# One core, attention and a gated feed-forward layer: the last batch's keys and queries turned over by DMA, four forms of products told apart by the planner, the fourth batch's scores in steps of four banks

## The chip, the core and the metric

The kernel runs on one core of one Trainium2 chip. A core has five engines that run their own streams of instructions and wait for each other by semaphores: TensorE (PE: matmuls, with PEld for the loading of its weights), VectorE (DVE), ScalarE (ACT), GpSimd (POOL) and SyncE (SP, which here only issues DMAs). The metric is the device time of one launch in microseconds. The kernel before took 404.94 us (median of 3 runs, 404.52 to 405.55).

## What is computed

Attention for 8 batches of 8 heads, 576 tokens of 64 features, with 16 "beacon" keys and values in front that every token sees; then a feed-forward layer with a gate on all 4608 tokens of 512 features.

```python
k_all = np.concatenate([beacon_k, k], axis=2)          # q, k, v: 8 x 8 x 576 x 64; beacons: 16 rows
scores = scale * np.matmul(q, k_all.transpose(0, 1, 3, 2))
scores = np.where(causal, -1000000000.0, scores)       # beacons are seen by all
a = softmax(scores)
x = np.matmul(a, v_all)                                # then heads side by side: 4608 x 512
gate = np.maximum(x @ w_gate, 0.0)                     # 512 x 1536
val = x @ w_val
out = gate * val @ w_out                               # 1536 x 512
```

All inputs and the output are float32 in the chip's main memory (HBM); products are made in bf16.

## The kernel before

**The order is worked out by a planner.** The kernel's Python text first describes its work as a list of tasks (`add`, L178), each with the engines that may run it, a cost in us, the tasks that it needs, the buffers that it holds and a priority. `Plan.order` (L186) then plays them against those costs and writes the instructions out in the order that comes of it; so each engine's stream is fixed, and on the chip the engines only wait for what they need. For each task the planner knows the earliest time `at` at which it could run. It takes the smallest `at`; among equals a mark called `late`, and then the priority. For TensorE `late` (L232) depends on the task's form, `part`: a task of the same form as the one before goes first (-1), and one that changes the form waits behind others (1) until it has been ready for `lazy` us. A change of form costs `SWITCH` in the plan.

**Forms.** TensorE's array is used whole (128*128) for the feed-forward products, for turnings (transposes as matmuls with an identity) and for fillers; in quarters (64*64) for scores; in halves (128*64) for values; and 128*32 for the scores of the last rows. The tasks carry `part=2` for scores (L751), `part=1` for values (L868) and for the last rows' scores (L796), and 0 for the rest. The values of the last rows (L862, "F") are whole-array products but carry 1 too. Values have `lazy=20` from the third batch on.

**Attention, batch by batch** (`new_batch` L493, `quad` L763, `last` L784). The 8 heads are 4 pairs; a quad is 2 pairs, so a batch has quads 0 and 1. Keys and queries of a pair come by one DMA on SP's queue in runs of 1 KB (four rows of 64 floats; L554), are rounded to bf16 on POOL (L514), turned over by four 128-column matmuls (L525) into a PSUM bank, and copied by ACT or DVE into the tiles `kT` or `qT` (L463, L465). The first 16 rows and the rows left over come by loads of their own (L607), values by rows in 256-byte runs (L644). Scores (L743) are made in steps that hold PSUM banks: `STEPS` has six small steps to a quad, `STEPS2` three large ones of four banks (two for each of two heads); `BIGSTEP` (L34) says from which batch on `STEPS2` is used: before, from batch 4, the fifth. Then the softmax: masks and minima on DVE (L691), exponentials on ACT (L698), reciprocals on DVE (L704), scaling on POOL (L709). The weights are turned over by a DMA transpose on SP's queue (L829), for the first batch by matmuls (L819); then come the values (L839, L862) and copies into `xT`, from which the feed-forward part reads.

**Feed-forward** (`ffn` L892). Tokens are taken in ten spans (240, 336, seven of 512, 448). For each, 12 times: gate (L900) and value (L905), four matmuls each; ACT takes the relu (L911), DVE the product (L916); then 12 matmuls for each 128 tokens give the output (L931), which is copied to one of three `osb` tiles and stored by SP (L945). A span begins when the attention of all its tokens is in `xT`.

**What sets the order at the start.** POOL issues nine weight DMAs (`weight` L475; 512 KB each in bf16 at the destination, 1 MB of float32 read), not before `W0` + `W_STEP` times their number in plan time (L479). `HELD` (L38) keeps a load of the second batch, and those after it, behind the issue of a weight: the entry `(1, 3): ('v', 0, 0)` holds load 3 of batch 1 until the first w_val piece has been issued, through a one-element memset on POOL (L535). The loads' order in a batch is "KQ0011v2233vvvv" (L651): 0 and 1 are rests, 2 and 3 pair 0, 4 and 5 pair 1. `BEHIND` (L39) holds a load behind the scaling of a quad. `AFTER` and `PACE` (L61, L62) set the plan time from which a quad's scores may run: with 39, quad g of batch b from 39 * (b + g/2) on. Where the plan leaves TensorE idle before 160 us, fillers (L990), products that nobody reads, are put in.

Of the kernel before, what the change touches and what calls it, by code (L numbers as in the profile page):

```python
# [17 lines left out]


BACKLOG = 4.0  # L20
RANK1 = -10.0
AHEAD = 2.0
WWORK = -15.0
FILLED = 160.0
# [5 lines left out]
LAGS = {"PE": 0.22, "ACT": 0.16, "DVE": 0.14, "POOL": 0.1, "DMA": 0.1}  # L30
LAZY = 20.0
LAZY1 = 0.0
ON_PE = 2
BIGSTEP = 3  # L34
PEQ = lambda b, g: b < 1
ENG = [("POOL", "DVE"), ("POOL",), ("POOL",)]
F_MOST = 3
HELD = {(1, 3): ('v', 0, 0), (1, 5): ('g', 0, 512), (1, 11): ('o', 0, 0)}  # L38
BEHIND = {(2, 7): (1, 1)}  # L39
MARK = 0.08  # L40
AB_FIRST = 0
W_FIRST = 0
# [4 lines left out]
ORDER0 = ("k00", "q00", "K", "Q", "k10", "q10", "v", "v", "k01", "q01", "k11", "q11", "v", "v", "v")  # L47
W_COLS = [(0, 512), (512, 512), (1024, 512)]
W_ROWS = 4
W0 = 16.5  # L50
W_STEP = 3.4
W_ISSUE = 0.85
W_MOVE = 0.72
V_MOVE = 1.25
LAND = 1.8
N_ST = 8
N_OSB = 3
FIRST_SPANS = [240, 336]
LAST_SPAN = 448
FIRST_MOST = 3  # L60
AFTER = [[0.0, 8.0]]  # L61
PACE = 39.0  # L62


class Slots:
# [104 lines left out]
class Plan:  # L170
# [7 lines left out]
    def add(self, engines, cost, run, deps=(), holds=(), prio=0.0, lag=None, part=0, lazy=0.0, after=0.0, move=0.0):  # L178
        t = Task(engines if isinstance(engines, tuple) else (engines,), cost, run, deps, holds, prio, lag, part, lazy, move)
        t.ready = after  # L180
        for d in t.deps:
            d.users.append(t)
        self.tasks.append(t)
        return t

    def order(self):  # L186
# [11 lines left out]
        part = 0  # L198
# [23 lines left out]
        while True:  # L222
            best = None
            for e in queue:
                for t in queue[e]:
                    times = begin(t, e)
                    if times is None:
                        continue
                    at, could = times
                    late = 0  # L230
                    if e == "PE":
                        late = -1 if part and t.part == part else 1 if part != t.part and at < t.ready + t.lazy else 0  # L232
                    key = (at, late, t.prio)
                    if best is None or key < best[0]:
                        best = (key, t, e)
            if best is None:
                break
            (at, _, _), t, e = best
            for x in t.engines:
                queue[x].remove(t)  # L240
            for h in t.holds:
                if h.tile is None:
                    if h.next is not None:
                        h.tile, h.next.tile = h.slots.take_pair()
                    else:
                        h.tile = h.slots.take()
            if e == "PE" and FILL_FROM < at < self.filled:
                since, tile = max(free[e], FILL_FROM), self.filler
                if at >= FILL_BANK:
                    first = min(self.banks.free, key=lambda f: f[:2], default=(at, 0, None))  # L250
                    since, tile = max(since, first[0]), first[2]
                n = int((at - since) * FILL / (0.11 if at > FILL_COLD else 0.22))
                if n > 0 and tile is not None:
                    done.append(Filler(n, tile, self.fill))
            t.start, t.engine = at, e
            cost = t.cost
            if e == "DMA":
                issue, move = cost
                if issue > 1.2:
                    wire = max(wire, at + 0.3) + move  # L260
                    free[e] = max(at + issue, wire - 0.2)
                else:
                    free[e] = at + issue
                    wire = max(wire, at + issue) + move
                end = max(wire, free[e]) + LAND
            else:
                if isinstance(cost, dict):
                    cost = cost[e]
                if e == "PE":
                    cost += SWITCH * (t.part != part)  # L270
                    part = t.part
                free[e] = end = at + cost
                if t.move:
                    wire = max(wire, end) + t.move
                    end = wire + LAND
            for h in t.holds:
                h.users -= 1
                if h.users == 0:
                    h.slots.give(end + (0.1 if e == "DMA" else LAGS[e] if t.lag is None else t.lag), h.tile)
            done.append(t)  # L280
            for u, then in [(u, end) for u in t.users] + [(u, free[e]) for u in t.soon]:
# [11 lines left out]
def kernel(  # L293
# [12 lines left out]
    nc = tc.nc  # L306
    B, H, S, D = q.shape
    Nb = beacon_k.shape[2]
    DM = H * D
    NT = B * S  # L310
# [182 lines left out]
    def new_batch(b, prio, work):  # L493
# [24 lines left out]
        def turned(h16, rows, ca, prio):  # L518
            ps = Hold(first_ps if b == 0 else v_ps, 2)

            def turn(_):
                for a in range(4):

                    to = ps.tile[:, a * P:a * P + rows]
                    nc.tensor.matmul(to, h16.tile[:rows, a * P:(a + 1) * P], ident[:rows, :rows], start=True, stop=True)  # L525

            return ps, add("PE", c_pe(4 * rows), turn, (ca, on_ident), (h16, ps), prio[1])
# [20 lines left out]
        def load_pair(kind, p, prio):  # L548

            src, s0 = {"k": (k, 0), "q": (q, 64 - Nb)}[kind]  # L550
            st = staged()

            def fetch(_):
                nc.sync.dma_start(st.tile.rearrange("p (h e) -> p h e", h=2),  # L554
                                  src[b, bass.ds(4 * (p // 2) + p % 2, 2, step=2), s0:s0 + MAIN, :].rearrange("h (p j) d -> p h (j d)", j=4))

            ld = add("DMA", (0.5, 0.87), fetch, (held,), (st,), prio[0])
            dst = t.kT if kind == "k" else t.q
            h16, ca = rounded(dst, st, P, neg_scale if kind == "q" else 1.0, prio, ld,
                              lambda to, src: [(  # L560
                to.rearrange("p (j h d) -> p h j d", h=2, j=4), src.rearrange("p (h j d) -> p h j d", h=2, j=4))])
            zeros = on_zeros.get(b) if kind == "q" else None
            ps, tu = turned(h16, P, ca, prio)
            c0 = Nb if kind == "k" else 64
# [149 lines left out]
    def quad_scores(t, g, step, phs, vals, prio, after):  # L714
# [34 lines left out]
        for x in banks[0] + banks[1]:  # L749
            x.users += 1  # L750
        s = add("PE", sum(x[2] for x in cols) / 2400.0 + 0.03, scores, deps, (*banks[0], *banks[1], *[phs[k] for k in ks], t.kT, t.q), prio, None,  # L751
                part=2, after=after)
        parts = [[], []]
        for k in ks:
            phs[k].users += 1
# [28 lines left out]
    def last(t, prio):  # L784

        ph = Hold(p_s[0], 1)
        sc = [Hold(first_sc if t.b == 0 else sc_s, 4) for _ in range(2)]
        sc[0].next, sc[1].prev = sc[1], sc[0]
        deps = [x for key, made in t.rows.items() if key[0] in "kq" for x in made]
        def scores(_):  # L790
            for bank, a, n in ((sc[0], 0, 512), (sc[1], 512, SK - 512)):
                for pp in range(NP):
                    nc.tensor.matmul(bank.tile[32 * pp:32 * pp + 32, :n], t.q.tile[:, pp, S + Nb - TAIL:],
                                     t.kT.tile[:, pp, a:a + n], start=True, stop=True)

        s = add("PE", SK / 2400.0 + 0.05, scores, deps, (*sc, ph, t.kT, t.q), prio, None, part=1)  # L796
        parts = [(SK, tuple(sc), 0, mask_f, SK - 512, on_mask_f, 0, s)]
        outs = softmax(t, parts, ph, prio, 0)
        ph.users += 1 + len(outs)
        finish(t, 0, ("F",), ph, pT_s[0], NC, [list(range(NC))] if t.b < ON_PE else [], outs, prio)  # L800

    def finish(t, p, vals, ph, pt_s, blocks, on_pe, outs, prio):
# [30 lines left out]
        def one(what):  # L833
# [8 lines left out]
            def values(_):  # L842
# [15 lines left out]
                else:  # L858
                    for pp in range(NP):
# [6 lines left out]
            nv = 2 if what == "AB" else NC  # L866
            pe = {"AB": 0.17, "CDE": 0.54, "F": 0.45}[what]
            va = add("PE", pe, values, tr + [t.rows["v", c] for c in range(nv)], (pt, ps, t.v), prio - 5, None,  # L868
                     part=1, lazy=LAZY if t.b > 1 else LAZY1 * t.b)

            def to_x(x):
                pv = ps.tile
# [99 lines left out]
    spans = []  # L972
    for w in FIRST_SPANS:
        spans.append((sum(spans[-1]) if spans else 0, w))
    end = NT - LAST_SPAN
    while sum(spans[-1]) < end:
        a = sum(spans[-1])
        spans.append((a, min(MT, end - a)))
    spans.append((end, NT - end))
    for i, (m0, mt) in enumerate(spans):  # L980
        deps = []
        for b in range(B):
# [41 lines left out]
```

## Time and profile before

| | us |
|---|---|
| median of 3 runs | 404.94 |
| lowest, highest | 404.52, 405.55 |
| the profiled execution | 405.02 |
| its span (first to last instruction) | 403.3 |
| PE busy | 388.6 |
| DVE, ACT, POOL busy | 294.8, 260.3, 233.9 |
| SP's DMA queue (q1): packet time as a share of 16 engines' span | 72.7% |

The profiled execution is 0.08 us above the median, and 1.7 us of it lie outside the span. Busy times are the union of an engine's instructions. Durations of matmuls overlap, since they are pipelined: what one costs is the distance from its start to the next one's.

### The profile page before, as it was taken

To read this page: it belongs to the slowest core of one execution; us is meant where nothing else is said; L and a number is where in the kernel's file an instruction comes from. 1 tells how busy PE (TensorE), PEld (TensorE's weight loads), DVE (VectorE), ACT (ScalarE), POOL (GpSimd) and SP (SyncE) were. 2 spreads that over 40 slices of the span, in tenths; PEclk is the share of its full clock that TensorE was granted. 3 is DMA by queue.
4 is the path that set the end of the run, shared out by engine and by line. 5 is a ranking of instruction groups with operands and counts; after the bars stand their busy time and mean duration, and the time that the engine had idled before them with its cause. 6 is when DMAs were issued, how large, how long until landed. Compare 5 with 4: busy or idle time off the path is not lost.

```text
span 403.3 us, 9980 instructions
## 1 busy us (share of the span) xinstructions
PE 388.6 (96%) x3276; PEld 205.8 (51%) x3316; DVE 294.8 (73%) x1046; ACT 260.3 (65%) x814; POOL 233.9 (58%) x453
## 2 busy tenths in 40 slices
PE   6999999999999999999999999999999999999994
PEld 4657855545444546455545444544454454444542
DVE  3899899896989897788797969797868633333331
ACT  2998798895877687769676878496848621320310
POOL 6899979796769469586758676676443320000000
PEclk9999999999999999999999999999999999999999
DMA  7999989999999999899999969792829074002002
GB/s 186 202 239 227 242 138 228 184 213 258 211 228 217 185 207 216 183 267 252 167 195 286 216 152 238 218 221 47 164 78 192 0 138 133 0 0 98 8 2 92
DMA packets 173476, 67.83 MB, mean 168 GB/s; under 512 B 145712, under 2 KB 168880, under 8 KB 173424
## 3 DMA queue, kind: packets, MB, share of 16 engines
q1 hardware_dynamic: 168592, 62.41, 72.7%
q0 software_dynamic: 4752, 4.72, 7.2%
q8 instruction: 26, 0.43, 0.4%
q14 instruction: 26, 0.21, 0.2%
q10 hardware_dynamic: 80, 0.07, 0.1%
HBM read 38.54 MB, written 9.44 MB: 119 GB/s over the span
## 4 chain that ended last, share of the span: by engine, by line
PE 85%; DMA 6%; POOL 3%; DVE 2%; ACT 1%; issue 1%; SPq 1%; DVEq 0%
PE f L931 23%; PE f L905 22%; PE f L900 21%; PE f L839 6%; PE f L743 6%; PE f L525 4%; DMA wv_r<-in_moe_w_val_dram 2%; DMA pTb<-pb 2%; POOL pb L709 1%; DMA st<-in_q_dram 1%; PE f L819 1%; ACT xT L698 1%; PE f L862 1%; PE f L990 1%; DVE f L691 1%
## 5 line engine op out<-in xcount | busy, mean ns | idle before, releaser
L709 POOL TENSOR_SCALAR pb<-pb,small 128x384 bf16<-128x384 bf16 (+8 forms) x272 | 141.5, 539 | 74.1 <-DVE small L704 73.4
L698 ACT ACTIVATE pb<-f,small 128x448 bf16<-128x448 f32 (+8 forms) x272 | 143.9, 554 | 27.4 <-DVE small L691 23.9
L691 DVE CUSTOM_DVE_ANT_0 f<-f,mask 128x576 f32<-128x576 f32 (+8 forms) x288 | 134.3, 513 | 13.6 <-PE f L743 9.6
L905 PE MATMUL f<-xT,wv_r 128*128 128x512 bf16 (+3 forms) x466 | 106.3, 358 | 2.3 <-DMA wv_r<-in_moe_w_val_dram 1.0
L900 PE MATMUL f<-xT,wg_r 128*128 128x512 bf16 (+3 forms) x471 | 105.2, 358 | 0.7 <-DMA wg_r<-in_moe_w_gate_dram 0.4
L916 DVE TENSOR_TENSOR hT<-g,f 128x512 bf16<-128x512 f32 (+3 forms) x120 | 75.1, 632 | 38.0 <-PE f L905 35.1
L911 ACT ACTIVATE g<-f 128x512 f32<-128x512 f32 (+3 forms) x120 | 67.0, 564 | 55.0 <-PE f L900 50.7
L931 PE MATMUL f<-wo_r,hT 128*128 128x512 bf16 (+3 forms) x439 | 98.8, 374 | 1.6 <-issue 1.1
L900 PEld LDWEIGHTS <-wg_r 128*128 128x128 bf16 x480 | 45.1, 98 | 44.3 <-issue 1.5
L905 PEld LDWEIGHTS <-wv_r 128*128 128x128 bf16 x480 | 43.8, 98 | 44.5 <-issue 5.1
L931 PEld LDWEIGHTS <-hT 128*128 128x128 bf16 (+2 forms) x456 | 41.9, 100 | 46.9 <-issue 2.9
L698 ACT ACTIVATION_READ_ACCUMULATOR pb<-f,small 128x1 f32 x272 | 60.8, 224 | 0.0
L514 POOL TENSOR_SCALAR h<-st 128x512 bf16<-128x512 f32 (+1 forms) x93 | 49.1, 542 | 12.1 <-DMA st<-in_k_dram 4.0
L691 DVE DVE_READ_ACCUMULATOR2_ANT small<- 128x1 f32 x296 | 41.9, 142 | 0.1
L465 DVE COPY osb<-f 128x512 f32<-128x512 f32 (+3 forms) x32 | 21.9, 683 | 26.1 <-PE f L931 25.9
L743 PE MATMUL f<-kT,qT 64*64 64x512 bf16 (+7 forms) x640 | 34.8, 295 | 0.1
L525 PE MATMUL f<-ident,h 128*128 128x128 bf16 (+1 forms) x320 | 28.1, 221 | 1.4 <-POOL h L514 1.2
L704 DVE RECIPROCAL small<-small 128x1 f32<-128x1 f32 (+3 forms) x144 | 22.0, 161 | 8.9 <-ACT pb L698 6.4
L525 PEld LDWEIGHTS <-h 128*128 128x128 bf16 (+1 forms) x320 | 21.3, 100 | 14.0 <-POOL h L514 3.2
L743 PEld LDWEIGHTS <-qT 64*64 64x64 bf16 x640 | 14.4, 106 | 23.1 <-issue 18.6
L839 PE MATMUL f<-pTb,v 128*64 128x320 bf16 (+3 forms) x488 | 25.7, 253 | 0.5 <-DMA pTb<-pb 0.5
L839 PEld LDWEIGHTS <-v 128*64 128x64 bf16 (+1 forms) x512 | 20.9, 109 | 8.9 <-issue 4.5
(61 smaller groups left out, 233.8 us busy)
## 6 DMA issues: line engine op xcount, KB each, us to landing
out_dram<-osb SPq DMA_DIRECT2D x34, 256.0 KB, 2.5
st<-in_k_dram SPq DMA_DIRECT2D x32, 256.0 KB, 4.1
st<-in_q_dram SPq DMA_DIRECT2D x32, 256.0 KB, 4.5
st<-in_v_dram SPq DMA_DIRECT2D x24, 256.0 KB, 5.8
st<-in_v_dram SPq DMA_DIRECT2D x8, 224.0 KB, 4.9
wg_r<-in_moe_w_gate_dram POOLq DMA_DIRECT2D x3, 512.0 KB, 7.4
wv_r<-in_moe_w_val_dram POOLq DMA_DIRECT2D x3, 512.0 KB, 7.6
wo_r<-in_moe_w_out_dram POOLq DMA_DIRECT2D x3, 512.0 KB, 7.6
```

Of the source, the lines that this page charges most:

```text
L514: (nc.gpsimd if x.engine == "POOL" else nc.vector).tensor_scalar(to, src, by, 1.0, ALU.mult, ALU.mult)
L525: nc.tensor.matmul(to, h16.tile[:rows, a * P:(a + 1) * P], ident[:rows, :rows], start=True, stop=True)
L691: nc.vector.tensor_tensor_reduce(out=view(i, n - m), in0=view(i, n - m), in1=msk, scale=1.0, scalar=at(7) if m < n else 3.0e38, op0=ALU.ad ...
L698: nc.scalar.activation(ph.tile.rearrange("p a n -> p (a n)")[:, a:a + n], view(i), AF.Exp, bias=at(i), scale=-1.0, accum_out=at(4 + i))
L709: nc.gpsimd.tensor_scalar(one, one, at(8 + i), 1.0, ALU.mult, ALU.mult)
L743: nc.tensor.matmul(banks[k][b_].tile[64 * i:64 * i + 64, off:off + n], t.q.tile[r, 2 * g + i, 64 * j:64 * j + 64], t.kT.tile[r, 2 * g + i, ...
L839: nc.tensor.matmul(ps.tile[64 * hh:64 * hh + 64, d0:d0 + w], t.v.tile[:rows, c, D * h:D * h + D], rhs(64 * hh), start=(c == 0), stop=(c == ...
L900: nc.tensor.matmul(psg.tile[:, :mt], wg_r[:, ki, nf * P:(nf + 1) * P], xT[:, ki, m0:m0 + mt], start=(ki == 0), stop=(ki == KM - 1))
L905: nc.tensor.matmul(psv.tile[:, :mt], wv_r[:, ki, nf * P:(nf + 1) * P], xT[:, ki, m0:m0 + mt], start=(ki == 0), stop=(ki == KM - 1))
L911: r = add("ACT", c_act(mt), lambda _, psg=psg, g=g: nc.scalar.activation(g.tile[:, :mt], psg.tile[:, :mt], AF.Relu), (a,), (psg, g), -1000 ...
L916: hid.append(add("DVE", c_dve(mt), lambda _, psv=psv, g=g, nf=nf: nc.vector.tensor_mul(hT[nf].tile[:, :mt], g.tile[:, :mt], psv.tile[:, :m ...
L931: nc.tensor.matmul(ps[c].tile[64 * c:64 * c + rows, :w], hT[nf].tile[:, t0:t0 + rows], wo_r[:, nf, w * c:w * c + w], start=(nf == 0), stop ...
```

## The change

Constants of the planner:

```diff
-RANK1 = -10.0
+RANK1 = -14.0
...
+SLAZY = 0.0
+NEXT = -0.5
 ON_PE = 2
-BIGSTEP = 3
+TURN = (7,)
+TURN_FIRST = 100
+TURN_LOAD = 1.5
+BIGSTEP = 2
...
-HELD = {(1, 3): ('v', 0, 0), (1, 5): ('g', 0, 512), (1, 11): ('o', 0, 0)}
-BEHIND = {(2, 7): (1, 1)}
+HELD = {(1, 0): ("v", 0, 0), (1, 2): ("g", 0, 1024), (1, 4): ("v", 0, 1024)}
+BEHIND = {(2, 2): (1, 0), (2, 7): (1, 1)}
...
-W0 = 16.5
-W_STEP = 3.4
+W0 = 14.0
+W_STEP = 1.4
...
-FIRST_SPANS = [240, 336]
-LAST_SPAN = 448
+SPANS = [240, 336, 512, 512, 512, 512, 512, 512, 512, 448]
 FIRST_MOST = 3
-AFTER = [[0.0, 8.0]]
-PACE = 39.0
+AFTER = [[0.0, 12.0]]
+PACE = 38.0
```

The spans come out the same as before, now from a list. The order of TensorE's tasks, in `Plan.order`:

```diff
-                        late = -1 if part and t.part == part else 1 if part != t.part and at < t.ready + t.lazy else 0
+                        late = -1 if part and t.part == part else NEXT if part and t.part else 1 if part != t.part and at < t.ready + t.lazy else 0
```

From one form of attention products the planner thus goes to another one that is ready before it goes back to whole-array products. The last rows' scores become `part=3`, their values `part=0`:

```diff
-        s = add("PE", SK / 2400.0 + 0.05, scores, deps, (*sc, ph, t.kT, t.q), prio, None, part=1)
+        s = add("PE", SK / 2400.0 + 0.05, scores, deps, (*sc, ph, t.kT, t.q), prio, None, part=3)
...
-                     part=1, lazy=LAZY if t.b > 1 else LAZY1 * t.b)
+                     part=0 if what == "F" else 1, lazy=LAZY if t.b > 1 else LAZY1 * t.b)
```

The last batch's pairs, in `load_pair`: two loads of 128 KB in 256-byte runs in place of one of 256 KB in 1 KB runs; the rounding keeps the columns' order; and one DMA transpose on SP's queue takes the place of four matmuls, a PSUM bank and a copy.

```diff
             def fetch(_):
+                if b in TURN:
+                    for i in range(2):
+                        nc.sync.dma_start(st.tile.rearrange("p (n h d) -> p h n d", h=2, d=D)[:, i],
+                                          src[b, 4 * (p // 2) + p % 2 + 2 * i, s0:s0 + MAIN, :].rearrange("(n p) d -> p n d", p=P))
+                    return
...
-            ld = add("DMA", (0.5, 0.87), fetch, (held,), (st,), prio[0])
+            ld = add("DMA", (1.0, TURN_LOAD) if b in TURN else (0.5, 0.87), fetch, (held,), (st,), prio[0])
...
+            c0 = Nb if kind == "k" else 64
+            if b in TURN:
+                t.rows[kind, p] = [add("DMA", (1.22, 0.177 * 4), lambda _: nc.sync.dma_start_transpose(
+                    dst.tile[:, p, c0:c0 + MAIN].rearrange("p (j n) -> p j n", j=4), h16.tile), (ca, zeros), (h16, dst), prio[0] - TURN_FIRST)]
+                return
```

More of the change, by code (lines that the diff above doesn't have):

```diff
@@ L553, in fetch @@
             def fetch(_):
+                if b in TURN:
[3 more added lines that the diff above has]
+                    return
                 nc.sync.dma_start(st.tile.rearrange("p (h e) -> p h e", h=2),
                                   src[b, bass.ds(4 * (p // 2) + p % 2, 2, step=2), s0:s0 + MAIN, :].rearrange("h (p j) d -> p h (j d)", j=4))
-            ld = add("DMA", (0.5, 0.87), fetch, (held,), (st,), prio[0])
+            ld = add("DMA", (1.0, TURN_LOAD) if b in TURN else (0.5, 0.87), fetch, (held,), (st,), prio[0])
             dst = t.kT if kind == "k" else t.q
             h16, ca = rounded(dst, st, P, neg_scale if kind == "q" else 1.0, prio, ld,
-                              lambda to, src: [(
+                              lambda to, src: [(to, src)] if b in TURN else [(
                 to.rearrange("p (j h d) -> p h j d", h=2, j=4), src.rearrange("p (h j d) -> p h j d", h=2, j=4))])
             zeros = on_zeros.get(b) if kind == "q" else None
+            c0 = Nb if kind == "k" else 64
[3 more added lines that the diff above has]
+                return
             ps, tu = turned(h16, P, ca, prio)
-            c0 = Nb if kind == "k" else 64
             def evict(x):
@@ L751, in quad_scores @@
         s = add("PE", sum(x[2] for x in cols) / 2400.0 + 0.03, scores, deps, (*banks[0], *banks[1], *[phs[k] for k in ks], t.kT, t.q), prio, None,
-                part=2, after=after)
+                part=2, after=after, lazy=SLAZY if t.b > 1 else 0.0)
         parts = [[], []]
@@ L971 @@
                 held.left += 1
[L972 to L979, printed above, removed]
+    spans = [(sum(SPANS[:i]), w) for i, w in enumerate(SPANS)]
     for i, (m0, mt) in enumerate(spans):
```

## The prediction

> **What bounds the kernel now.** I read the page's first lines first, for the busiest engine and for the chain that ended last.
>
> ```profile
> span 403.3 us, 9980 instructions
> PE 388.6 (96%) x3276; PEld 205.8 (51%) x3316; DVE 294.8 (73%) x1046; ACT 260.3 (65%) x814; POOL 233.9 (58%) x453
> PE 85%; DMA 6%; POOL 3%; DVE 2%; ACT 1%; issue 1%; SPq 1%; DVEq 0%
> ```
>
> PE is busy 96% of the span and makes 85% of the chain. Where is the rest? The table of windows (columns: length, then busy us and count of PE, PEld, DVE, ACT, POOL, then granted clock, DMA share, GB/s) and PE's waits say it.
>
> ```profile
> 10.00:20.00 10.00, 9.72 (x117) 6.75 (x116) 8.89 (x48) 9.67 (x39) 7.99 (x17) 1.00 1.01 204
> 20.00:30.00 10.00, 9.14 (x99) 5.56 (x97) 9.10 (x41) 9.93 (x34) 9.86 (x21) 1.00 1.20 237
> 30.00:40.00 10.00, 9.27 (x116) 7.04 (x116) 9.11 (x37) 8.57 (x22) 9.77 (x17) 1.00 1.21 227
> 60.00:80.00 20.00, 19.98 (x206) 12.10 (x206) 18.77 (x75) 17.27 (x58) 16.78 (x32) 1.00 1.01 197
> 80.00:100.00 20.00, 19.39 (x182) 10.31 (x182) 16.67 (x65) 15.05 (x49) 16.35 (x34) 1.00 1.13 238
> ...
> 300.00:320.00 20.00, 19.79 (x167) 9.70 (x167) 15.48 (x51) 13.01 (x41) 8.43 (x17) 1.00 0.59 109
> ```
> ```profile
> PE f L905 <- DMA wv_r<-in_moe_w_val_dram: 1.0, 2, 0.6
> PE f L839 <- DMA pTb<-pb: 0.5, 1, 0.5
> PE f L900 <- DMA wg_r<-in_moe_w_gate_dram: 0.4, 1, 0.4
> ```
>
> Two things are to be seen. From 60 us to the last products PE is busy 19.4 to 20.0 us of every 20, at a clock of 1.00, while POOL, and late in the run DVE and ACT too, have room: there the time is the sum of what PE is given, and whatever leaves PE's stream leaves the time. Before 40 us PE is not full; POOL is (9.86 and 9.77 of 10), and the DMA share is over 1. All waits of PE for weights, 1.4 us, lie in this start. The 0.5 us for `pTb` belongs to batch 1's values:
>
> ```profile
> 87.94 0.88 PE L839 MATMUL f<-pTb,v 128*64 128x128 bf16 x16 [0.46 <-DMA pTb<-pb]
> ...
> 92.40 0.88 PE L839 MATMUL f<-pTb,v 128*64 128x128 bf16 x16
> ...
> 94.11 1.03 PE L900 MATMUL f<-xT,wg_r 128*128 128x512 bf16 x3
> ```
>
> This is a second gate. At 94.11 span 2 begins, which needs the values of batch 1; those end at 93.3, and PE had nothing better to do ahead of 87.94 than wait. So feed-forward work done earlier in the start is of no use unless batch 1's values come earlier too. I call the moment 94.11 the hand-over.
>
> **The change, part by part.** All sums are made against the profiled execution, 405.02 us (403.3 of span and 1.7 around it, 0.08 above the median).
>
> *Turning by DMA.* Batch 7 loses 8 pairs of four 128-column matmuls. In the chain of waits twelve of them take 0.67 us, one after the other:
>
> ```profile
> 263.92 0.67 PE f L525 x12
> ```
>
> That is 56 ns each; 32 make **-1.79 us**. They have the feed-forward products' form, so no change of form goes with them. The eight copies leave ACT and DVE, which have room. The other side is SP and DMA:
>
> ```profile
> st<-in_k_dram SPq DMA_DIRECT2D x32, 256.0 KB, 4.1
> st<-in_v_dram SPq DMA_DIRECT2D x24, 256.0 KB, 5.8
> pTa<-pa SPq DMA_TRANSPOSE x6, 3.0
> ```
> ```profile
> L829 SPq DMA_TRANSPOSE pTa<-pa x6: 1202/1232/1292, 129.7 to 276.3; - x6
> ```
> ```profile
> L554 SPq DMA_DIRECT2D st<-in_k_dram x28: 367/445/2197, 18.9 to 254.8; - x28
> ```
>
> The values' loads have 256-byte runs already: 5.8 us to landing against 4.1. A five-block transpose (`pTa`) holds SP 1.23 us and lands after 3.0; the new ones have four blocks. SP thus gets 8 x 0.45 for the extra loads and 8 x 1.23 at most, 13.4 us in all, in front of batch 6's transposes, batch 7's values and the stores. A pair's load, rounding (0.6) and transpose take some 5.8 + 0.6 + 3.0 = 9.4 us, where load and rounding alone took 4.7. Who waits for that? Batch 7's scores, and batch 7 is not urgent:
>
> ```profile
> 337.52 1.50 PE f L839 x32
> 389.23 8.38 PE f L931 x56
> ```
>
> Its last values run at 337.52, and PE has feed-forward work from there to 397.6. That 58 us cover hides a delay of 10 us; without it each us would cost one. Stores held up can stall PE through the three `osb` tiles: between 0 and 2 us, nearest the wait list, where PE waits for none now; I take 0.
>
> The Trainium skill, "VectorE: DVE Perf Modes", section "Rules for kernel authors", speaks against this edit: a 128x128 transpose belongs on TensorE if PSUM will do. Its section "The three transpose paths" gives 390 ns there and 1309 ns by DMA; an estimate by that page is 32 x 0.39 = 12.5 us off PE and 42 us onto the DMA side. The trace has 56 ns for PE's place in the stream, so the gain is a seventh of that; the rule looks at the latency of one, and this kernel lacks PE time.
>
> *Fourth batch in large steps.* The price of a change of form comes from a stretch of timeline beside the chain:
>
> ```profile
> 206.95 1.03 PE L931 MATMUL f<-wo_r,hT 128*128 128x512 bf16 x4
> 207.91 0.63 PE L743 MATMUL f<-kT,qT 64*64 64x192 bf16 x12
> ```
> ```profile
> 344.31 1.73 PE f L905 x8
> 346.04 1.73 PE f L900 x8
> ```
>
> Unbroken, 512 columns take 1.73 / 8 = 0.216 us. Four take 0.865, but the scores begin 0.96 us after: a change costs 0.095 us. Quad 0 of batch 3 has four stretches of scores, that of batch 4 three; the first and the last of each are
>
> ```profile
> 119.37 0.63 PE L743 MATMUL f<-kT,qT 64*64 64x64 bf16 x16
> ...
> 129.21 0.56 PE L743 MATMUL f<-kT,qT 64*64 64x512 bf16 x12
> ```
> ```profile
> 157.61 0.63 PE L743 MATMUL f<-kT,qT 64*64 64x64 bf16 x16
> ...
> 172.04 0.55 PE L743 MATMUL f<-kT,qT 64*64 64x512 bf16 x12
> ```
>
> Two quads lose one stretch each, two changes a stretch: 4 x 0.095 = **-0.38 us**. Four banks must be free together, so scores come a little later; as in batch 4, feed-forward work covers that.
>
> *Four forms.* After scores PE now goes straight to ready values, or the reverse: one change saved where the two would have stood apart. But values no longer wait up to 20 us, so two pairs that went as one stretch (x32 at 337.52) may go as two, each behind scores: nothing is won there. Batches 2 to 7 have 12 quads. The gain lies between 0 and 12 x 2 x 0.095 = 2.3 us; I take six or seven changes, **-0.6 us**, nearer the lower end because of the splitting. "F" values as whole-array products no longer wait for a change they don't make: within the same bound.
>
> *The start.* The weights' earliest issues go from 16.5, 19.9, ... to 14.0, 15.4, ...; loads of batch 1 are held behind the issues of the second, fifth and sixth. The windows of the fillers' line alone show what stands between the first feed-forward products:
>
> ```profile
> 26.00:30.00 4.00, 0.59 (x3) 0.20 (x2) 1.00 1.22 264
> 30.00:34.00 4.00, 1.66 (x9) 0.72 (x9) 1.00 1.21 235
> ```
>
> Were weights never late, 1.4 us of waits and some 1.3 of these twelve fillers (0.59 + 1.66 less their overlap) could hold work. Only an earlier hand-over cashes that. What sets it?
>
> ```profile
> 41.86 1.78 POOL L514 TENSOR_SCALAR h<-st 128x512 bf16<-128x512 f32 x3
> ...
> 44.87 1.20 POOL L514 TENSOR_SCALAR h<-st 128x512 bf16<-128x512 f32 x2 [0.65 <-PE f L525]
> 46.01 0.79 POOL L477 DMA_DIRECT2D wo_r<-in_moe_w_out_dram  x1
> ...
> 47.56 0.79 POOL L477 DMA_DIRECT2D wo_r<-in_moe_w_out_dram  x1
> ```
>
> Batch 1's keys and queries are rounded at 41.86 and 44.87 on a full POOL. Two weight issues that now stand behind them, 2 x 0.79, move in front: up to +1.6 us. Against that, `PACE` lets batch 1's second quad go 1.5 us earlier (57 for 58.5) and every later one more. From -2.7 to +1.6, I take **-0.5**. `RANK1`, the list of spans and `AFTER` change no order that the trace lets me see: 0. The pace beyond the hand-over moves work among engines with room, and PE's sum stays.
>
> Sum: -1.79 - 0.38 - 0.6 - 0.5 = -3.3 us; 405.02 - 3.3 = **401.7 us**.
>
> **Rivals.** *The gain is lost at the hand-over or to split values* (0.17): turnings and steps give 2.2 us, the forms nothing, and the two weight issues in front of batch 1 cost 1.6: 404.4. For it speaks that POOL has no room from 20 to 40; against it that it had 2 us of idle in 10 to 20.
>
> *The hand-over comes late* (0.26), the slower end. Loads from batch 1's pair 1 on wait for the sixth weight's issue and queue behind six transfers.
>
> ```profile
> q0 software_dynamic: 4752, 4.72, 7.2%
> ```
> ```profile
> 36.61 0.79 POOL L477 DMA_DIRECT2D wv_r<-in_moe_w_val_dram  x1
> ```
>
> By q0's share nine weights take 0.072 x 403.3 = 29 us of 16 engines, 3.2 each; six from 14 us on end at 33, in a DMA system already over 1.2. Pair 1 then lands at 38 to 41, and must be there by 41.9, when POOL takes it now. It decides when the sixth issue slips to its present 36.61: landing at about 42 to 45 (4.1 us and a transfer of 3.2 ahead, with values behind), batch 1 up to 5 us late, PE dry at 94. Price: 405.0 - 2.8 + 5 = 407.2. Against it: an issue asked for at 14.0 + 5 x 1.4 = 21 us has 15 us in hand.
>
> *The hand-over comes early by all 2.7 us* (0.09): 399.5. *The change doesn't do what it says* (within the forecast's chance): no values join scores, only turnings and steps count: 402.9.
>
> **How the numbers follow.** Forecast 0.48. Its own range, with the forms at 0 to 2.3 and the start at -1.5 to +0.5, is 399.0 to 403.4. The first rival has 0.17, the second 0.26, the third 0.09. The range that holds 8 in 10 takes in the price of the late hand-over: 399.2 to 407.2. This kernel's measurement tells about 0.3%, 1.2 us, from no change: faster means below 403.7, slower above 406.2. Faster: the forecast, the early hand-over and 0.01 of the first rival, 0.58. Same: the first rival's other 0.16 and 0.02 of the late hand-over, 0.18. Slower: its other 0.24.
>
> **What would show it.** Right: L525 has 32 matmuls fewer; PE's busy time falls by some 3 us; batch 3 has six stretches of scores; more values stand directly behind scores; no new PE wait between 230 and 340 us, and span 2's first gate product at 94 or earlier. Wrong: that product at 96 or later with PE waiting for `pTb` or scores before it; PE waits behind `osb` while SP issues batch 7's transposes; batch 7's values within a few us of the end.

## The result and the profile after

| us | before | after |
|---|---|---|
| median (8 runs each) | 404.73 | 399.75 |
| lowest, highest | 403.36, 406.24 | 398.15, 402.93 |
| the profiled execution | 405.02 | 399.48 |
| its span | 403.3 | 397.8 |

The ratio is 0.9896, with a 95% interval of 0.9867 to 0.9924: the changed kernel is 4.2 us faster by the ratio (3.1 to 5.4), and its median lies 5.0 lower. The forecast was 401.7, in a range of 399.2 to 407.2. The spread within the changed kernel goes with TensorE's granted clock: its five runs up to 400.03 us show a mean clock of 0.998 or more, the three from 401.53 us on 0.991 to 0.994.

The first lines of the page and PE's share of the chain, after:

```profile
span 397.8 us, 9897 instructions
PE 386.6 (97%) x3235; PEld 203.8 (51%) x3278; DVE 287.6 (72%) x1024; ACT 261.7 (66%) x820; POOL 234.2 (59%) x454
PE 88%; POOL 3%; DVE 3%; DMA 2%; issue 1%; SPq 1%; ACT 0%; POOLq 0%; ACTq 0%
```

PE is busy 2.0 us less in a span 5.5 us shorter, so the other 3.5 us were time in which PE stood idle. Where was it? The same windows as before (length, busy us and count of PE, PEld, DVE, ACT, POOL, clock, DMA share, GB/s):

```profile
20.00:30.00 10.00, 9.36 (x103) 6.08 (x101) 9.34 (x40) 9.73 (x33) 9.87 (x19) 1.00 1.23 205
30.00:40.00 10.00, 9.87 (x126) 7.12 (x124) 9.71 (x38) 9.54 (x28) 9.90 (x20) 1.00 1.11 228
60.00:80.00 20.00, 19.94 (x190) 11.72 (x190) 17.42 (x72) 17.88 (x61) 17.40 (x35) 1.00 0.92 197
80.00:100.00 20.00, 19.84 (x197) 10.29 (x199) 17.09 (x66) 14.99 (x53) 14.46 (x29) 1.00 1.02 251
```

From 20 to 40 us PE went from 18.41 to 19.23 us, from 60 to 100 from 39.37 to 39.78: 1.2 us of gaps are closed ahead of the hand-over or near it. The fillers' line alone, in the two stretches in which twelve fillers stood before:

```profile
26.00:30.00 4.00, 0.12 (x2) 0.00 (x0) 1.00 1.21 198
30.00:34.00 4.00, 0.00 (x0) 0.00 (x0) 1.00 1.06 170
```

Ten of them gave way to work (four come back later, up to 87.9 us). The list of PE's waits has neither a weight nor `pTb` any more:

```profile
PE f L996 <- POOL mask L415: 2.0, 1, 2.0
PE f L529 <- POOL h L518: 1.4, 3, 0.8
PE f L832 <- POOL xT L722: 0.6, 1, 0.6
PE f L944 <- issue: 0.5, 3, 0.2
```

The last stretch of products before, then, after, batch 1's values, span 2's first gate product and the last stretch (time of start, duration):

```profile
389.07 8.50 PE L931 MATMUL f<-wo_r,hT 128*128 128x512 bf16 x56
```
```profile
84.92 0.88 PE L852 MATMUL f<-pTb,v 128*64 128x128 bf16 x16
...
89.34 0.88 PE L852 MATMUL f<-pTb,v 128*64 128x128 bf16 x16
...
91.61 1.04 PE L913 MATMUL f<-xT,wg_r 128*128 128x512 bf16 x3
...
385.17 8.50 PE L944 MATMUL f<-wo_r,hT 128*128 128x512 bf16 x56
```

The hand-over comes at 91.61 for 94.11, 2.5 us earlier. Not all of that is won, for a little less work stands ahead of it. The traces have 112 turnings of keys and queries there for 120, and 194 of the quads' score products for 200. Eight turnings are 0.45 us at 56 ns each; the six score products, which ran as part of x12 at 89.95 before, now run at 92.80 and hold PE for 0.48 us. So some 0.9 us are only put off, and **1.6 us** are won at the hand-over. The last products, 8.50 us long in both kernels, began at 389.07 before and begin at 385.17 now. That is 3.9 us, which leaves **2.3 us** for the stream after the hand-over (1.4 by these times, and the 0.9 that it took over). The span shrank by 5.5: the other **1.6 us** lie behind the last product. Here are the last stores, on ACT's queue (time of issue, its duration), first of the kernel before, then of the changed one:

```profile
398.04 2.41 ACTq L945 DMA_DIRECT2D out_dram<-osb  x1
```
```profile
394.14 0.57 ACTq L958 DMA_DIRECT2D out_dram<-osb  x1
```

The same instruction took 2.41 us to issue and takes 0.57 now. The change says nothing of it; it is taken up with the experiments.

### The profile page after: what moved, and what is told of

It reads as the page before. It is cut to its first block, busy times and chain, and to the rows that moved or that the text cites. A ratio compares the mean times of both kernels' runs of the same rounds, so it can differ in the third digit from the quotient of the medians.

```text
span 397.8 us, 9897 instructions
## 1 busy us (share of the span) xinstructions
PE 386.6 (97%) x3235; PEld 203.8 (51%) x3278; DVE 287.6 (72%) x1024; ACT 261.7 (66%) x820; POOL 234.2 (59%) x454
## 4 chain that ended last, share of the span: by engine, by line
PE 88%; POOL 3%; DVE 3%; DMA 2%; issue 1%; SPq 1%; ACT 0%; POOLq 0%; ACTq 0%
PE f L918 23%; PE f L944 23%; PE f L913 22%; PE f L756 7%; PE f L852 6%; PE f L529 3%; DMA st<-in_q_dram 2%; POOL xT L722 2%; DVE f L704 2%; PE f L832 1%; PE f L996 1%; PE f L875 1%; PE f L806 1%; DVE osb L469 1%; POOL h L518 1%
## 5 line engine op out<-in xcount | busy, mean ns | idle before, releaser
L722 POOL TENSOR_SCALAR pb<-pb,small 128x448 bf16<-128x448 bf16 (+8 forms) x272 | 141.5, 539 | 70.5 <-DVE small L717 69.8
L711 ACT ACTIVATE pb<-f,small 128x320 bf16<-128x320 f32 (+8 forms) x272 | 143.9, 553 | 22.6 <-DVE small L704 17.7
L469 DVE COPY osb<-f 128x512 f32<-128x512 f32 (+2 forms) x32 | 21.7, 682 | 28.1 <-PE f L944 27.7
L467 ACT CAST xT<-f 128x240 bf16<-128x240 f32 (+2 forms) x56 | 21.2, 385 | 30.7 <-PE f L852 29.5
L717 DVE RECIPROCAL small<-small 128x1 f32<-128x1 f32 (+3 forms) x136 | 20.9, 161 | 13.5 <-ACT pb L711 9.8
L529 PE MATMUL f<-ident,h 128*128 128x128 bf16 (+1 forms) x288 | 26.8, 222 | 1.6 <-POOL h L518 1.4
L529 PEld LDWEIGHTS <-h 128*128 128x128 bf16 (+1 forms) x288 | 20.0, 101 | 14.6 <-POOL h L518 4.0
L852 PE MATMUL f<-pTb,v 128*64 128x320 bf16 (+3 forms) x488 | 26.7, 253 | 0.0
L471 POOL TENSOR_SCALAR v<-st 128x512 bf16<-128x512 f32 (+1 forms) x38 | 23.2, 617 | 4.0 <-DMA st<-in_v_dram 4.0
```

Of the source, the lines that this page charges most:

```text
L711: nc.scalar.activation(ph.tile.rearrange("p a n -> p (a n)")[:, a:a + n], view(i), AF.Exp, bias=at(i), scale=-1.0, accum_out=at(4 + i))
L722: nc.gpsimd.tensor_scalar(one, one, at(8 + i), 1.0, ALU.mult, ALU.mult)
L852: nc.tensor.matmul(ps.tile[64 * hh:64 * hh + 64, d0:d0 + w], t.v.tile[:rows, c, D * h:D * h + D], rhs(64 * hh), start=(c == 0), stop=(c == ...
```

## The experiments

**The theories.** Mine: the gain is the sum of the prediction's parts, with a larger start. Rivals: the forms carry it (they are what lets the new start work); the start is worth nothing and the pace is; the tail is the source of a part that no edit was meant to touch. Each part was undone in the changed kernel or put alone into the one before. Every ratio is to the kernel before, over the same runs of a chip. A difference of two such ratios, with intervals of 0.0026 to 0.0029 each way, is known to about 0.004, 1.6 us; 1% is 4.05 us.

**Turning alone, in the kernel before**: `TURN = (7,)` with the code that it needs.

> The kernel before with the turning by DMA alone. Theory 'sum of PE': 1.8 us less for 32 matmuls, 0.2 us more for two changes of form: 1.6 us faster than before (0.996). Rival 'SP's queue': transposes hold up stores and batch 7's values, PE shows waits between 230 and 340 us, time within 0.5 us of before or slower.

Measured: 0.9964 (0.9938 to 0.9991), 403.32: 1.5 us faster.

**Everything but the turning:**

```diff
-TURN = (7,)
+TURN = ()
```

> The changed kernel with the turning by DMA taken out (batch 7's pairs are loaded in 1 KB runs and turned over by TensorE again). Theory 'sum of PE': 32 matmuls of 56 ns come back, 1.8 us slower than the changed kernel, some 2.5 us faster than before (ratio about 0.994); the hand-over (first 512-column gate product) stays at 91.6 us. Rival 'hidden': those matmuls lay where PE had slack, and the time stays that of the changed kernel, about 4.5 us faster than before (0.989).

Measured: 0.9960 (0.9934 to 0.9987), 402.95: of the change's 0.0104 the turning takes 0.0064 with it, 2.6 us. The two answers, 1.5 and 2.6, stand on either side of the sum's 1.79. In both pairs the last store is issued alike, so that issue has no part in either. The hand-over of the kernel without the turning comes at 93.47 in its profiled execution, where 91.6 was expected. The order of its work is the same up to there; but 3.41 us at half the clock, from 18.10 on, stand in the start of that execution (see the last section).

**Large steps from the fifth batch only, as before:**

```diff
-BIGSTEP = 2
+BIGSTEP = 3
```

> The changed kernel with batch 3's scores in six small steps again. The stream has 198 changes of form against 184. Theory 'sum of PE': 14 x 0.095 = 1.3 us slower than the changed kernel. Rival 'only four changes count, as predicted': 0.4 us slower. Rival 'large steps cost a wait for four banks': faster than the changed kernel.

Measured: 0.9919 (0.9892 to 0.9946), 402.32: 0.9 us more than the changed kernel. The sign is that of the first two theories; the size can't be told from nothing. The trace has 198 changes of form here against 184. Its hand-over, 93.82, again follows a stretch at half the clock.

**The forms alone, in the kernel before:** the new rule in `Plan.order`, `part=3` for the last rows' scores and 0 for their values.

> The kernel before with the new rule for the order of forms alone (and the new marks of the last rows' products). The stream has 189 changes of form against 188. Theory 'sum of PE': no fewer changes, no gain, within 0.5 us of before. Rival 'forms move the hand-over': values come earlier in batch 1, hand-over at 92 to 93 us, 1 to 2 us faster than before.

Measured: 0.9988 (0.9965 to 1.0011), 404.81: nothing. The trace has 190 changes of form (189 were expected) against 188. The hand-over comes at 92.69, as the rival had it, but with 48 output products recorded ahead of it for 57, and the time does not follow.

**Everything but the forms:**

```diff
-late = -1 if part and t.part == part else NEXT if part and t.part else 1 if part != t.part and at < t.ready + t.lazy else 0
+late = -1 if part and t.part == part else 1 if part != t.part and at < t.ready + t.lazy else 0
...
-                      part=0 if what == "F" else 1, lazy=LAZY if t.b > 1 else LAZY1 * t.b)
+                      part=1, lazy=LAZY if t.b > 1 else LAZY1 * t.b)
```

(and `part=3` back to 1).

> The changed kernel with the old rule for the order of forms and the old marks of the last rows' products. Its stream has 193 changes of form against 184 and 162 fillers against 88. Theory 'sum of PE, forms save changes': 9 changes at 0.095 us, 0.9 us slower than the changed kernel, and the fillers only fill what is idle anyway. Rival 'forms move the hand-over': the 74 fillers more stand where PE lacks work because values come later, up to 74 x 0.107 = 8 us slower, with a hand-over later than 93 us.

Measured: 1.0316 (1.0282 to 1.0349), 417.78: 17 us more than the changed kernel. Neither theory had that price. Where does it stand? Not at the hand-over, which comes at 91.18: 65 of the fillers run behind it. PE's timeline of this kernel shows fillers far behind the start, where PE should be full:

```profile
137.12 3.45 PE L996 MATMUL f<-mask,ident 128*128 128x256 bf16 x30
140.50 0.88 PE L852 MATMUL f<-pTb,v 128*64 128x128 bf16 x16
...
141.87 3.34 PE L996 MATMUL f<-mask,ident 128*128 128x256 bf16 x29
146.94 0.88 PE L852 MATMUL f<-pTb,v 128*64 128x128 bf16 x16 [1.72 <-ACT pb L711]
```

PE had run out of feed-forward products, because batch 2 was late. SP's queue of the same kernel, then of the changed one:

```profile
65.93 0.51 SPq L563 DMA_DIRECT2D st<-in_k_dram  x1
68.12 16.59 SPq L842 DMA_TRANSPOSE pTb<-pb  x4
...
86.29 1.35 SPq L563 DMA_DIRECT2D st<-in_k_dram  x1
```
```profile
63.62 8.16 SPq L842 DMA_TRANSPOSE pTb<-pb  x2
72.33 0.41 SPq L563 DMA_DIRECT2D st<-in_k_dram  x1
...
76.43 5.07 SPq L842 DMA_TRANSPOSE pTb<-pb  x1
```

In the changed kernel batch 2's first pairs are loaded behind two transposes, at 72.33; here only at 86.29, behind four of them, 16.59 us of SP's queue in one piece. (The loads ahead of the four, to 65.93, are batch 3's, which are not held.) Batch 2's pairs are held by `BEHIND`'s new entry `(2, 2): (1, 0)` until batch 1's quad 0 has been scaled. The one-element memset that releases them ran on POOL at 65.12 there and at 70.81 here, after the first of the four transposes had begun. With a release 5.7 us later the loads come 14.0 us later; their place in SP's queue was settled when the planner wrote the streams. So the theory: it is the hold that costs, not the forms. The same kernel without the hold tells them apart:

```diff
-BEHIND = {(2, 2): (1, 0), (2, 7): (1, 1)}
+BEHIND = {(2, 7): (1, 1)}
```

> The changed kernel with the old rule for the order of forms and the old marks, as in a_oldforms, and without the entry (2, 2): (1, 0) of BEHIND, which holds batch 2's pair loads behind the scaling of batch 1's quad 0. Its stream has 90 fillers against 162 and 189 changes of form. Theory 'held loads': in a_oldforms batch 3's loads overtook batch 2's, which then stood behind four transposes; without the entry that is gone, and the time is 0.5 us above the changed kernel plus what the hand-over loses, ratio 0.990 to 0.997. Rival 'late values': the old rule itself holds values back, so the time stays near a_oldforms, ratio above 1.02.

Measured: 0.9977 (0.9957 to 0.9996), 404.50, a little above the top of what was expected. 13.7 of the 17 us are gone with one entry. Four transposes stand in a row in this kernel too (16.90 us from 69.00 on), but batch 2's first pairs are loaded ahead of them: so the row of four is not by itself what cost the time, and the loads behind it are the difference. The 3.3 us that are left are the price of the forms and of the hold together. Much of it lies in the start. With early weights, but without the hold and the new forms, the hand-over comes at 94.56, with about as much work ahead of it as in the changed kernel; so the weights do not bring it nearer by themselves.

**Everything but the start:** `RANK1`, `HELD`, `BEHIND`, `W0`, `W_STEP` and `AFTER` as before; `PACE` stays at 38.

> The changed kernel with the start's constants as before (RANK1, HELD, BEHIND, W0, W_STEP, AFTER); pace 38, forms and turning stay as changed. Theory 'early weights bring the hand-over nearer': it goes back to 94 us, 2 to 2.5 us slower than the changed kernel, plus 6 changes of form, 0.6 us. Rival 'the pace and the new order of forms bring it': the hand-over stays within 0.5 us of 91.6, time within 1 us of the changed kernel.

Measured: 0.9944 (0.9917 to 0.9970), 402.58: 1.9 us more than the changed kernel. Its profiled execution, 406.48, lies 3.9 above its median and has 3.41 us at half the clock from 31.93 on; it is not used for the place of the hand-over.

**The start alone, in the kernel before:** the same constants, nothing else.

> The kernel before with the start's constants alone (RANK1, HELD, BEHIND, W0, W_STEP, AFTER). The stream has 197 changes of form against 188 and 112 fillers against 94. Theory 'early weights bring the hand-over nearer': it comes at 92 us, 2 us less, 0.9 us more for the changes: about 1 us faster than before. Rival 'start, pace and forms only work together': hand-over at 94 us or later, 1 us or more slower than before.

Measured: 1.0150 (1.0122 to 1.0177), 411.24: 6.1 us slower than before. The hand-over comes at 91.00, even a little earlier than the theory had it, but with 160 of the quads' score products ahead of it for 200: batch 2 is late, and the early hand-over buys nothing. This has the sign of the late rival, and SP's queue shows the same picture as under the old forms:

```profile
77.33 8.27 SPq L829 DMA_TRANSPOSE pTb<-pb  x2
86.53 0.37 SPq L554 DMA_DIRECT2D st<-in_q_dram  x1
```

A load of batch 2's queries stands behind two transposes, the batch's scores begin at 93.9 (83.2 in the changed kernel), and after the hand-over 20 fillers run where the changed kernel has none. That the hold does it here too is argued from these rows; it was not tried.

**The pace as before:**

```diff
-PACE = 38.0
+PACE = 39.0
```

> The changed kernel at the old pace, 39. The stream has 194 changes of form against 184 and the same 88 fillers. Theory 'the start's weights bring the hand-over nearer': it stays at 91.6 to 92, and only 10 changes, 0.95 us, are added. Rival 'the pace brings it nearer': batch 1's second quad is released 1.5 us later, hand-over at 93 to 94, 2 to 3 us slower than the changed kernel.

Measured: 0.9914 (0.9886 to 0.9942), 401.65, with a hand-over at 91.39 and the same work ahead of it: 0.7 us more than the changed kernel, within what can't be told apart. The early hand-over is not the pace's work.

**More turning:** batches 6 and 7, and 5 to 7.

```diff
-TURN = (7,)
+TURN = (6, 7)
```

> The changed kernel with batch 6's pairs turned by DMA as well. 32 matmuls fewer, 185 changes of form against 184, 88 fillers as before. Theory 'sum of PE': 1.7 us faster than the changed kernel, ratio to before about 0.985. Rival 'SP's queue': batch 6's keys come late behind other transposes, scores or values wait, no gain or a loss, 0.989 or more.

Measured: 1.0407 (1.0371 to 1.0444), 421.83: 21 us more than the changed kernel, where 32 turnings fewer would have won 1.8. PE's waits, then SP's turnings and loads, then the windows:

```profile
PE f L852 <- DMA pTb<-pb: 15.5, 4, 9.0
```
```profile
215.06 1.19 SPq L574 DMA_TRANSPOSE kT<-h  x1
...
253.64 1.21 SPq L574 DMA_TRANSPOSE qT<-h  x1
...
269.13 0.63 SPq L620 DMA_DIRECT2D st<-in_k_dram  x1
...
273.12 0.97 SPq L560 DMA_DIRECT2D st<-in_k_dram  x2
```
```profile
340.00:345.00 5.00, 0.00 (x0) 0.00 (x0) 0.00 (x0) 0.00 (x0) 0.77 (x2) 0.50 0.80 149
345.00:350.00 5.00, 1.60 (x18) 1.09 (x20) 0.90 (x2) 0.00 (x0) 0.00 (x0) 0.50 0.97 179
```

Batch 6's eight turnings are spread over 38.6 us of SP's queue, in order among `pTb` transposes; batch 7's pairs are loaded at 273.12 (237.97 in the changed kernel), its values are not ready when the feed-forward work is out, and PE stands still from 340 to 345 at half the clock, and is still at half when it goes on.

> The changed kernel with the pairs of batches 5, 6 and 7 turned by DMA. 64 matmuls fewer (3.6 us), 175 changes of form against 184 (0.85 us), 88 fillers. Theory 'sum of PE': 4.4 us faster than the changed kernel, ratio about 0.979. Rival 'SP's queue': 27 us more of SP time than in the kernel before, stores and transposes late, no gain or a loss.

Measured: 1.0694 (1.0663 to 1.0725), 433.87: the third batch costs 12 us more, by the same waits (18.5 us for `pTb`).

**The tail:** in the kernel before, the very last store goes by SP's queue like all others.

```diff
-                    q_ = nc.scalar if c else nc.sync
+                    q_ = nc.sync
```

> The kernel before with its one store on ACT's queue (the second half of the last rows) issued by SP instead. Theory 'code loading': in the trace of before this issue took 2.41 us, with a load of code 0.6 us after its start; in the changed kernel it took 0.57. On SP the last two stores stand in a row, some 0.6 us, and the tail gets shorter by 1 us or more: ratio about 0.997. Rival 'landing': the tail is the landing of the last data whoever issues it, and the ratio is 1.000.

Measured: 0.9956 (0.9941 to 0.9972), 403.62: 1.8 us faster (1.1 to 2.4). One line without any change in the work gives as much as the whole turning. In its profiled execution the end lies 4.7 us after the last product's start, for 6.0 before, so the landing of the last data does not set the tail alone.

None of the twelve variants beat the changed kernel. That kernel with all stores on SP's queue was not tried; its last store issues in 0.57 us already.

## Why the prediction was right, and where it was not

**Right in sign and within its range, but in part by another sum.** In the profiled pair the time fell by 5.5 us, where 3.3 were forecast. With the work put off counted where it runs, the start gave 1.6 for 0.5, the stream after the hand-over 2.3 for 2.8 (2.2 without the forms), and the tail 1.6 for 0. PE's busy time fell by 2.0 us, where some 3 were named as a sign. That the time fell within the range is in part luck: the tail's 1.6 us had no term, the start was mis-sized by 1.1, and the forms' 0.6 came to nothing.

*Turning by DMA, -1.79: held.* The trace has the 32 matmuls fewer (before, then after), and turning alone in the kernel before, and all but the turning in the changed one, gave 1.5 and 2.6 us:

```profile
L525 PE MATMUL f<-ident,h x320: 197/219/314, 4.6 to 264.4; 128*128 128x128 bf16 x128, 80*128 80x80 bf16 x32
```
```profile
L529 PE MATMUL f<-ident,h x288: 197/219/314, 4.4 to 243.0; 128*128 128x128 bf16 x112, 80*128 80x80 bf16 x32
```

The cover held as well. The turnings of batch 7 went to SP from 252.00 to 293.61:

```profile
252.00 1.22 SPq L574 DMA_TRANSPOSE kT<-h  x1
...
293.61 1.21 SPq L574 DMA_TRANSPOSE qT<-h  x1
```

One transpose holds SP 1.22 us, as the sum had it (1.23 from five blocks), but from the first to the last of the eight went 42 us, because the queue's order puts them among loads and `pTb` transposes of some 4.2 us each. All the same, batch 7's two quads began their scores at 275.49 and 297.97 (280.06 and 301.98 before), its last values came at 333.56 (337.52 before), and no wait of PE stands there: they kept the 4 us that the whole kernel had moved forward. The Trainium skill, "VectorE: DVE Perf Modes", section "Rules for kernel authors", puts a 128x128 transpose on TensorE. By the runs the rule loses for batch 7, whose scores can wait (ratio 0.9964 for that edit alone). With batch 6 turned as well it wins: batch 6's delay is passed on to batch 7, which then can't wait, and 21 us are lost. Batch 6 alone was not tried.

*Fourth batch in large steps, -0.38: right in sign.* Batch 3 has six stretches of scores, where it had eight, so the four changes are gone as counted. Undoing the edit cost 0.9 us, with 1.6 either way; between 0.38, the 1.3 of fourteen changes of form and nothing the runs can't choose.

*Four forms, -0.6: wrong; it is nothing.* This step failed: "I take six or seven changes". I had named the reason for less, the splitting, and not counted it through. The rule does what it says, as PE's timeline shows at the end of batch 5's scores and the start of batch 6's:

```profile
231.68 0.55 PE L756 MATMUL f<-kT,qT 64*64 64x512 bf16 x12
232.16 0.88 PE L852 MATMUL f<-pTb,v 128*64 128x128 bf16 x16
...
238.26 0.63 PE L756 MATMUL f<-kT,qT 64*64 64x64 bf16 x16
238.82 0.88 PE L852 MATMUL f<-pTb,v 128*64 128x128 bf16 x16
```

Values go directly behind scores 15 times after the hand-over, where they never did. But one stretch of x32 by itself costs two changes, and two stretches of x16 behind scores cost one each: the same two. In all, stretches of values went from 14 to 20, and changes of form from 188 to 184: no more than the four counted for the large steps. The forms alone changed nothing that could be measured (404.81 for 404.90), while their profiled execution has the quick last store (0.58 us). So they may cost PE's stream what the tail gave; a single profiled execution can't settle it. Whether the new start needs them is open: without them, but with the hold, batch 2 came late.

*The start, -0.5: right in sign, too small.* This step failed: "Two weight issues that now stand behind them move in front: up to +1.6 us". They still stand behind them. POOL's timeline, after:

```profile
41.65 1.19 POOL L518 TENSOR_SCALAR h<-st 128x512 bf16<-128x512 f32 x2
...
43.55 1.35 POOL L518 TENSOR_SCALAR h<-st 128x512 bf16<-128x512 f32 x2
44.84 0.79 POOL L481 DMA_DIRECT2D wo_r<-in_moe_w_out_dram  x1
...
47.27 0.79 POOL L481 DMA_DIRECT2D wo_r<-in_moe_w_out_dram  x1
```

I had taken the earliest times in the plan for the order on the engine. The sixth weight did come earlier, at 31.39 for 36.61, and the waits for weights are gone. The second source, which I had not seen, is what runs among batch 1's softmax. The transposes of its second quad begin at 79.37 before and at 76.43 after, 2.9 us earlier, and the values follow (84.92 for 87.94). First POOL and SP of the kernel before, then POOL of the changed one:

```profile
71.37 0.62 POOL L514 TENSOR_SCALAR h<-st 128x512 bf16<-128x512 f32 x1
...
78.14 1.20 POOL L709 TENSOR_SCALAR pb<-pb,small 128x576 bf16<-128x576 bf16 x2 [2.42 <-DVE small L704]
```
```profile
79.37 9.11 SPq L829 DMA_TRANSPOSE pTb<-pb  x2
```
```profile
74.43 1.20 POOL L722 TENSOR_SCALAR pb<-pb,small 128x576 bf16<-128x576 bf16 x2 [1.15 <-DVE small L717]
...
78.87 1.78 POOL L518 TENSOR_SCALAR h<-st 128x512 bf16<-128x512 f32 x3
```

Before, the transposes follow the end of the scaling (78.14 + 1.20 = 79.34) by 0.03 us. The scaling is late: three roundings of batch 2's first pairs (67.02, 68.06, 71.37), with their turnings on PE and copies on ACT and DVE, run among batch 1's softmax. After, no pair of batch 2 is rounded before 78.87, and the scaling is done at 75.63; SP, which issues batch 2's loads until 76.31, then takes 0.8 us of this back. What keeps batch 2's pairs away is `BEHIND`'s new hold, the same that cost 14 us under the old forms. That the hold brings the hand-over nearer is argued from these rows and from the kernel without it (hand-over at 94.56); it was not taken out of the changed kernel by itself.

Put back to the old start, the kernel lost 1.9 us, with 1.6 either way. The profiled executions bear the shift out. Three kernels that are the same up to the hand-over (before, turning alone, last store by SP) show it at 94.11, 94.72 and 93.38. Four with the new start and forms, the same work ahead of it and the full clock up to there (changed, pace as before, batches 6 and 7, batches 5 to 7) show it at 91.61, 91.39, 91.37 and 91.95. That is 2.5 us between the two means, the 0.9 put off included.

*The tail, not in the prediction: 1.6 us in the profiled pair.* The prediction put it at nothing without a word on it. No edit was meant to touch it; see the last section.

*The late rival* did not come by its own way, the sixth weight. Its sign came in two kernels, by `BEHIND`'s hold and SP's order (shown in one, argued in the other): an edit that I had costed within the start without a line of its own. In the changed kernel the release comes 5.7 us earlier than under the old forms, and there the hold does no such harm.

**Open.** The parts don't add up: 2.6, 0.9 and 1.9 us taken out singly and 1.6 of tail make 7.0, of 4.2 measured; with 1.6 either way on each that is no contradiction, and no proof of the shares either. Why batch 1's quad 0 is scaled 5.7 us later under the old rule was not followed to its cause, and which of the three marks of the forms matters was not tried.

## What to carry to other kernels

In-order queues that carry both loads and long transposes are where an edit's price hides: ask of each held load which transposes it will stand behind if its release slips, since here, with a release 6 us later, one hold cost 14 us. Work that leaves the bounding engine for such a queue pays while nothing waits for the batch behind it; the same edit on one batch more, the one before, turned 1.8 us of gain into 21 of loss. When a rule saves a change of form by joining stretches, count the stretches that it splits as well, and look at what stands behind the last product before a gain is put down to the edit. When a milestone in the trace comes earlier, count the work ahead of it: part of it may only have been put off, as 0.9 of 2.5 us were here.

## What the runs showed of the hardware

**The last store's issue.** In three of the thirteen kernels whose last store goes by ACT's queue (before, turning alone, batches 6 and 7) that issue took 2.41, 2.27 and 2.18 us; in the other ten 0.57 to 0.58. In those three, and in them alone, the trace has a load of 8 KB of code on the queue of instructions q14 0.5 to 0.6 us after the issue began (at 398.64 in the kernel before). With the last store on SP the kernel before gained 1.8 us. That ACT ran out of loaded code just there is argued from the times of these rows; no run shows it by itself. The Trainium skill, "Runtime: NRT & Kernel Launch", section "Instruction fetch mechanics", calls the cost of crossing into the next block of code mostly hidden; if these loads are such crossings, 1.6 to 1.8 us were not hidden here, and the measurement decides.

**The clock after a standstill.** The granted clock stood at 0.50 from 340 to 350 us in the kernel that turned batches 6 and 7, after PE had begun to starve. The whole stretch at 0.5 lasts 17.1 us (335.69 to 352.76). Apart from the last microseconds of every run, four other profiled executions have one short stretch at 0.5, of 3.41 us each: from 18.10 on without the turning, from 31.93 with the old start, from 192.12 under the old forms, and from 26.23 with large steps from the fifth batch only:

```profile
22.00:26.00 4.00, 2.56 (x27) 1.51 (x26) 4.00 (x19) 3.47 (x10) 3.51 (x7) 1.00 1.23 211
26.00:30.00 4.00, 3.92 (x27) 2.46 (x27) 2.30 (x13) 2.56 (x9) 3.80 (x7) 0.57 1.22 203
```

The mean of 0.57 over 4 us is that of 3.4 us at 0.5 and the rest at 1.0; 17.1 us are five such pieces. Ahead of each short stretch PE had idled: here 2.56 of 4 us are busy, with no gap longer than 0.61 us; in the other three one gap of 2.1 to 3.2 us stands there. Two of the four stretches lie ahead of a hand-over that can be compared: it comes at 93.47 and 93.82, some 2 us later than in the four executions with the same order of work and the full clock. The Trainium skill, "TensorE: Matmul & The Clock Gate", Part 1, gives a window of about 3.4 us after which an idle PE falls to half rate; the traces agree with its length. If an idle window means one without any product, the row from 22 to 26 us does not bear that out; how much idling is enough was not measured.
